# Products of a fused attention and gated feed-forward kernel for two pairs at once in half of the first stages, with a new order of steps

## The chip, the cores and the metric

The kernel runs on one core of one Trainium2 chip. The metric is the device time of one execution in microseconds (us), as the median of several runs. About 1% is what a measurement of this kernel can tell from no change.

## The reference

Attention over chunks of 64 positions (8 batches, 8 heads, 576 positions, head size 64), and behind it a feed-forward part without activation. All inputs and the output are float32; the kernel computes in bfloat16 with float32 sums.

```python
scores = scale * np.matmul(q_c, k_c.transpose(0, 1, 2, 4, 3))   # chunk by chunk
attn = softmax(scores)
out = np.matmul(attn, v_c)
x = out.transpose(0, 2, 1, 3).reshape(4608, 512)
a = x @ w1            # 512 -> 1024
b = x @ w2            # 512 -> 1024
h = a * b @ w3        # 1024 -> 1024
return h @ w_out      # 1024 -> 512
```

## The kernel before, in words

The 4608 tokens are cut into 18 pairs (p = 0 to 17) of 256 tokens (two units u of 128 tokens, each of two chunks). Two pairs make a couple of 512 tokens (g = p // 2). The product of w3 and w_out is made once in the kernel (steps V, W, Z), so that each couple needs one output product with `w3o` (512 columns).

There is no scheduler. A list in the text `ORDER` (lines 9 to 41) names every step, and the loop in lines 468 and 469 issues them in that order. Each engine works through its own instructions strictly in this order (`inorder`, line 92), and waits by semaphores for the data and buffers of others. So a step's place in the list is its place behind the earlier steps of the same engine only. The letters, with their functions:

- R (line 137) loads pair 0's raw q and k through the queues of SyncE (SP) and ScalarE (ACT); K casts them on ACT. q, k, v (lines 152 and 170), i (a quarter of w1 and of w2, 256 columns each, line 449), h (half of w3) and o (w_out) are loads on GpSimd's (POOL's) queue. A DMA here casts from float32 to bfloat16.
- T (line 201): transposes of q (T p.0) or k (T p.1) on VectorE (DVE). From pair 6 on, G (line 211, eight DMAs per couple on SP's queue) moves their 32-row blocks to other partitions, into `qkm`.
- S (line 220): the scores on TensorE (PE), 64 small matmuls for pairs 0 to 5, 32 from pair 6 on. E (line 237): the exponential on ACT. P (line 244): the product with v and a column of ones on PE.
- N (line 266): reciprocal of the sum and scaling on DVE, for unit 0 or 1. X (line 301): transpose of the result on DVE, into `xt` for pairs 0 to 5, else into `xm`, from which H (line 318, eight DMAs per couple on SP) moves it into `xt`.
- A and B (lines 361 to 366, through `do_AB`): x*w1 and x*w2 into the two banks of one PSUM tile (PSUM is the accumulation memory). C (line 368) copies the first from PSUM to SBUF on ACT; M (line 374) multiplies it with the second on DVE, into `ab`.
- O (line 398): output product, 16 matmuls of 512 columns on PE; Y: its copy on ACT; Q: its store on SP's queue.
- D (line 326): filler matmuls of zeros on PE, 9, 6 and 6 of 512 columns in the first stage.

A PSUM tile `p` of two banks is shared by S, P, A/B, W and O, and there are four of them (line 90); the buffers of q and k are five, of `ab` three, of `a_sb` three.

In `do_AB` before, a step A p.j of pairs 0 to 3 works for that pair alone: two blocks of 128 columns of w1 (f = 2j and 2j+1), four matmuls each over 256 tokens, eight matmuls with 256 columns (j = 0 to 3). From pair 4 on the steps stand at the even pairs only and work for a couple: one block f = j, four matmuls with 512 columns (j = 0 to 7).

```python
        fs = (f,) if p >= 4 else (2 * j, 2 * j + 1)
        n = GT // len(fs)
```

Of the kernel before, what the change touches and what calls it, by code (L numbers as in the profile page):

```python
# [7 lines left out]

ORDER = """
R0.0 R1.0 R0.1 R1.1 v0 D0.0.1.9.512 K0.0 K1.0 T0.0.0 K0.1 T0.1.0 K1.1 S0.0 T0.0.1 E0.0 T0.1.1 q1 k1  # L10
S0.1 i0 E0.1 P0.0 P0.1 T1.0 D0.1.0.6.512 v1 N0.0 T1.1 N0.1 X0.0 X0.1 i1 i2 S1 E1 D1.0.0.6.512 A0.0
C0.0 P1 B0.0 q2 N1.0 X1.0 N1.1 A0.1 C0.1 k2 B0.1 M0.0 A0.2 X1.1 A1.0 i3 C0.2 B0.2 M0.1 A1.1 v2 q3
B1.0 B1.1 M0.2 C1.0 C1.1 T2.0 k3 A0.3 C0.3 T2.1 S2 E2 B0.3 M1.0 M1.1 P2 M0.3 N2.0 N2.1 A1.2 C1.2
X2.0 A1.3 X2.1 C1.3 T3.0 B1.2 q4 T3.1 v3 k4 B1.3 A2.0 M1.2 C2.0 B2.0 S3 E3 T4.0 A2.1 M1.3 B2.1 M2.0
P3 A2.2 h0 N3.0 N3.1 B2.2 X3.0 A2.3 C2.1 C2.2 X3.1 o M2.1 C2.3 B2.3 A3.0 C3.0 M2.2 B3.0 V0 h1 A3.1
A3.2 q5 k5 C3.1 M2.3 B3.1 B3.2 v4 V1 C3.2 q6 T4.1 V2 V3 M3.0 W0 S4 k6 q7 M3.1 Z0 M3.2 V4 V5 W1 T5.0
Z1 W2 V6 V7 T5.1 W3 T6.0 E4 k7 q8 v5 Z2 A3.3 k8 q9 k9 Z3 S5 T6.1 T7.0 q10 T7.1 E5 v6 v7 C3.3 P4 B3.3
N4.0 X4.0 M3.3 O0 G3.0 N4.1 k10 Y0 G3.1 T8.0 O1 X4.1 P5 T8.1 Y1 O2 Q0 N5.0 N5.1 X5.0 v8 X5.1 A4.0 S6
E6 T9.0 T9.1 S7 B4.0 T10.0 Y2 q11 O3 C4.0 M4.0 Q1 E7 P6 v9 N6.0 A4.1 N6.1 C4.1 Y3 B4.1 A4.2 X6.0
M4.1 G4.0 A4.3 X6.1 C4.2 P7 N7.0 C4.3 B4.2 G4.1 k11 B4.3 N7.1 X7.0 A4.4 M4.2 B4.4 Q2 M4.3 C4.4 T10.1  # L20
M4.4 A4.5 C4.5 S8 B4.5 A4.6 C4.6 A4.7 E8 B4.6 Q3 C4.7 X7.1 B4.7 M4.5 q12 P8 H3.0 M4.6 S9 H3.1 M4.7
O4 E9 T11.0 Y4 P9 N8.0 O5 k12 N8.1 A6.0 B6.0 Y5 T11.1 G5.0 T12.0 A6.1 X8.0 N9.0 B6.1 C6.0 C6.1 T12.1
A6.2 q13 X8.1 B6.2 N9.1 X9.0 M6.0 k13 C6.2 v10 T13.0 v11 X9.1 M6.1 A6.3 M6.2 q14 G5.1 C6.3 A6.4 q15
B6.3 C6.4 B6.4 A6.5 S10 C6.5 B6.5 T13.1 M6.3 M6.4 A6.6 H4.0 E10 P10 H4.1 M6.5 S11 N10.0 B6.6 k14
N10.1 v12 A6.7 C6.6 E11 G6.0 P11 M6.6 N11.0 B6.7 X10.0 N11.1 A8.0 A8.1 B8.0 G6.1 C6.7 C8.0 B8.1 A8.2
B8.2 C8.1 M6.7 T14.0 q16 A8.3 M8.0 C8.2 M8.1 X10.1 M8.2 X11.0 Q4 q17 T14.1 H5.0 B8.3 C8.3 S12 S13
X11.1 A8.4 E12 C8.4 B8.4 k15 H5.1 M8.3 E13 v13 k16 A8.5 B8.5 P12 M8.4 k17 v14 T15.0 N12.0 N12.1 O6
A8.6 v15 C8.5 C8.6 T15.1 Y6 T16.0 B8.6 A8.7 M8.5 C8.7 P13 Q5 M8.6 B8.7 X12.0 A10.0 C10.0 B10.0 N13.0
N13.1 M8.7 G7.0 A10.1 T16.1 C10.1 A10.2 X12.1 X13.0 M10.0 C10.2 G7.1 B10.1 B10.2 A10.3 B10.3 C10.3
M10.1 T17.0 A10.4 C10.4 M10.2 M10.3 A10.5 T17.1 B10.4 M10.4 X13.1 v16 H6.0 S14 C10.5 S15 G8.0 B10.5  # L30
M10.5 O7 G8.1 E14 E15 P14 A10.6 H6.1 N14.0 C10.6 B10.6 A10.7 N14.1 Q6 Y7 M10.6 P15 N15.0 N15.1 C10.7
X14.0 S16 B10.7 M10.7 O8 E16 Q7 A12.0 B12.0 C12.0 M12.0 Y8 A12.1 C12.1 P16 S17 N16.0 X14.1 B12.1 E17
A12.2 M12.1 B12.2 A12.3 C12.2 A12.4 B12.3 X15.0 B12.4 v17 C12.3 M12.2 A12.5 N16.1 B12.5 M12.3 H7.0
X15.1 A12.6 X16.0 A12.7 C12.4 M12.4 C12.5 M12.5 C12.6 P17 N17.0 Q8 B12.6 B12.7 M12.6 H7.1 A14.0
A14.1 C12.7 B14.0 N17.1 C14.0 M12.7 O9 B14.1 C14.1 Y9 A14.2 X16.1 M14.0 M14.1 C14.2 A14.3 B14.2 Q9
O10 B14.3 X17.0 H8.0 Y10 Q10 A14.4 C14.3 A14.5 X17.1 C14.4 B14.4 M14.2 B14.5 H8.1 M14.3 A14.6 O11
Y11 B14.6 M14.4 O12 C14.5 C14.6 Y12 A14.7 M14.5 A16.0 C14.7 C16.0 Q11 M14.6 B14.7 A16.1 C16.1 A16.2
B16.0 B16.1 M14.7 M16.0 C16.2 M16.1 Q12 A16.3 O13 B16.2 B16.3 A16.4 C16.3 M16.2 Y13 M16.3 C16.4
A16.5 A16.6 B16.4 A16.7 C16.5 B16.5 M16.4 O14 Y14 C16.6 B16.6 C16.7 M16.5 B16.7 M16.6 Q13 M16.7 O15
Y15 O16 Q14 Q15 Y16 Q16 O17  # L40
"""


# [5 lines left out]
def first_path(  # L49
# [46 lines left out]
    def mm(*a, **kw):
        return inorder(nc.tensor.matmul(*a, **kw))  # L97
# [276 lines left out]
    def do_M(p, j):  # L374
        g = p // 2
        if g not in ab_t:
            ab_t[g] = msb.tile([P, FO, GT], bf, tag="ab", bufs=3, name="ab")
# [9 lines left out]
        inorder(nc.vector.tensor_mul(o, view(a_t.pop((p, j))[:]), view(ps_t.pop((p, j))[:, 1, :])))  # L387
# [201 lines left out]
```

## Time and profile before

| | |
|---|---|
| median of 3 runs | 242.46 us (241.17 to 243.07) |
| profiled execution: time | 241.66 us |
| profiled execution: span of its instructions | 240.1 us |
| mean granted TensorE clock | 0.985 |
| DMA moved | 39.21 MB, mean 163 GB/s |

The page's busy table gives each engine's busy time within the span. The views by stretch give, for a stretch of time, the busy time of an engine, the granted clock of TensorE (1.00 is full speed) and what the DMA engines moved. In a timeline a row has the start, the length, the engine, the line, the operation with output and input, the count, and in brackets the idle time ahead of it and what ended that. Names of tiles stand without buffer numbers, and all matmuls have line 97, the helper `mm`. A matmul tile that fillers allocated first is called `z_ps`, also where a score or a product goes into it later. A matmul's length holds its pipeline's drain, so the pace of a stream is read from start to start. A row's bracket names the releaser by what the profile infers.

### The profile page before, as it was taken

Reading aid. Unit: us, or ns where it says so; the run is one execution under the profiler, and the core shown is the slowest. Engines: PE = TensorE matmul, PEld = TensorE weight load, DVE = VectorE, ACT = ScalarE, POOL = GpSimd, SP = SyncE. Lnnn points to the kernel's source line nnn. Section 1 sums busy time; section 2 is a strip of 40 time slices with the busy share of each in tenths; the row PEclk is TensorE's granted clock in tenths of the full one; section 3 lists DMA queues with packets and bytes.
Section 4 is the critical chain, followed back from the end, with each engine's and each line's share of the span. In section 5 each row is a group of like instructions: output and inputs, shape, how many; then the busy total and the mean of one; then the engine's idle time right before and its main releaser. Section 6 shows DMA issues by size and latency. Waiting matters only on the chain.

```text
span 240.1 us, 6225 instructions
## 1 busy us (share of the span) xinstructions
PE 230.6 (96%) x2621; PEld 120.2 (50%) x2621; DVE 152.3 (63%) x237; ACT 84.7 (35%) x119; POOL 83.4 (35%) x112
## 2 busy tenths in 40 slices
...
GB/s 177 179 185 188 178 175 199 202 188 174 174 220 242 236 224 253 201 204 196 212 222 222 214 252 152 190 210 3 131 48 3 131 131 87 90 0 89 85 90 175
DMA packets 94397, 39.21 MB, mean 163 GB/s; under 512 B 75296, under 2 KB 86816, under 8 KB 94368
## 3 DMA queue, kind: packets, MB, share of 16 engines
...
q8 instruction: 20, 0.33, 0.5%
...
HBM read 38.80 MB, written 9.44 MB: 201 GB/s over the span
## 4 chain that ended last, share of the span: by engine, by line
PE 55%; DMA 31%; POOL 5%; DVE 3%; issue 2%; SPq 2%; ACT 1%; DVEq 0%; POOLq 0%
PE ab_ps L97 34%; PE o_ps L97 17%; DMA qk<-in_k_dram 17%; DMA w<-in_moe_w_dram 7%; DMA qk<-in_q_dram 4%; DMA qkm<-qkT 3%; POOL vbuf L100 2%; SPq L199 2%; PE s_ps L97 2%; POOL qk L100 2%; PE pv L97 2%; DVE ab L387 1%; POOL w L100 1%; DVE xn L272 1%; DVE qkT L207 1%
## 5 line engine op out<-in xcount | busy, mean ns | idle before, releaser
L97 PE MATMUL ab_ps<-xt,w 128*128 128x512 bf16 (+1 forms) x688 | 128.7, 342 | 0.5 <-DMA w<-in_moe_w_dram 0.5
L97 PEld LDWEIGHTS <-w 128*128 128x128 bf16 x704 | 67.0, 98 | 54.9 <-DMA w<-in_moe_w_dram 1.3
L387 DVE TENSOR_TENSOR ab<-a_sb,ab_ps 128x512 bf16<-128x512 f32 x71 | 47.0, 673 | 53.8 <-PE ab_ps L97 30.2
L370 ACT COPY a_sb<-ab_ps 128x512 f32<-128x512 f32 x71 | 41.4, 587 | 73.8 <-PE ab_ps L97 73.0
L97 PE MATMUL o_ps<-w3o,ab 128*128 128x512 bf16 (+2 forms) x296 | 64.8, 373 | 0.5 <-issue 0.3
L207 DVE STREAM_TRANSPOSE qkT<-qk 128x1024 bf16<-128x1024 bf16 (+1 forms) x38 | 45.8, 1232 | 5.5 <-ACT qk L150 3.7
L97 PEld LDWEIGHTS <-ab 128*128 128x128 bf16 x296 | 28.4, 98 | 33.6 <-issue 1.0
L100 POOL DMA_DIRECT2D vbuf<-in_v_dram x40 | 33.8, 847 | 23.2 <-DMA qk<-in_k_dram 5.9
L417 ACT COPY o_sb<-o_ps 128x1024 f32<-128x1024 f32 x17 | 17.2, 1014 | 43.8 <-PE o_ps L97 43.4
L272 DVE TENSOR_TENSOR xn<-pv,rcs 128x512 bf16<-128x512 f32 x36 | 24.9, 691 | 1.2
L100 POOL DMA_DIRECT2D qk<-in_q_dram x23 | 18.0, 783 | 15.8 <-DVE ab L387 4.8
L100 POOL DMA_DIRECT2D qk<-in_k_dram x23 | 17.9, 781 | 11.1 <-DMA qk<-in_k_dram 4.1
L240 ACT ACTIVATE e<-s_ps 128x1024 bf16<-128x1024 f32 (+1 forms) x17 | 16.9, 1000 | 11.4 <-PE s_ps L97 11.2
L313 DVE STREAM_TRANSPOSE xm<-xn 128x512 bf16<-128x512 bf16 x24 | 16.3, 689 | 0.1
L97 PE MATMUL w_ps<-wo,w3T 128*128 128x512 bf16 x64 | 14.1, 379 | 0.1
L269 DVE RECIPROCAL rcs<-pv 128x8 f32<-128x8 f32 x36 | 6.9, 192 | 11.4 <-PE pv L97 11.4
L291 POOL CROSS_LANE_REDUCE all_good<-good 128x1 f32<-128x1 f32 x1 | 0.4, 354 | 39.6 <-DVE both L289 39.6
L100 POOL DMA_DIRECT2D w<-in_moe_w_dram x16 | 11.1, 696 | 5.7 <-DMA w<-in_moe_w_dram 3.9
L97 PEld LDWEIGHTS <-e 64*32 64x32 bf16 (+1 forms) x768 | 7.8, 101 | 6.9 <-issue 4.4
L428 DVE STREAM_TRANSPOSE w3T<-w 128x1024 bf16<-128x1024 bf16 x8 | 9.5, 1210 | 2.4 <-DMA w<-in_moe_w_dram 2.4
L97 PE MATMUL pv<-vbuf,e 64*32 64x65 bf16 (+1 forms) x768 | 10.1, 198 | 0.3 <-ACT e L240 0.2
L97 PEld LDWEIGHTS <-w3T 128*128 128x128 bf16 x64 | 6.1, 98 | 7.5 <-issue 0.4
...
## 6 DMA issues: line engine op xcount, KB each, us to landing
...
qkm<-qkT SPq DMA_DIRECT2D x48, 128.0 KB, 7.0
vbuf<-in_v_dram POOLq DMA_DIRECT2D x32, 128.0 KB, 11.1
...
qk<-in_k_dram POOLq DMA_DIRECT2D x11, 256.0 KB, 12.1
...
```

What stands on the lines that cost most here:

```text
L97: return inorder(nc.tensor.matmul(*a, **kw))
L100: return inorder(nc.gpsimd.dma_start(dst, src))
L199: inorder(nc.sync.dma_start(dst, src))
L207: inorder(nc.vector.transpose(qkT_t[g][:, :, p % 2, s, heads(h)].rearrange("p e h (y t) -> p h t e y", t=2), qk_t[p][:, s, heads(h)].rearr ...
L240: inorder(nc.scalar.activation(e_t[p][:, :, heads(hh)], s_t[p, hh][:].rearrange("p u (h q) -> p u h q", q=CH)[:, :, heads(hh)], Exp, scale ...
L269: inorder(nc.vector.reciprocal(rc, pv[:, :, :, D:W]))
L272: inorder(nc.vector.tensor_mul(xn_t[p][:, u], pv[:, :, :, 0:D], rc.to_broadcast([P, 2, 4, D])))
L313: inorder(nc.vector.transpose(xm_t[g][:, u, :, m].rearrange("p o (c y) -> p c o y", y=BL), xn_t[p][:].rearrange("p u r m d -> p (u r) m d" ...
L370: first[p, j] = inorder(nc.scalar.copy(a_t[p, j][:], ps_t[p, j][:, 0, :]))
L387: inorder(nc.vector.tensor_mul(o, view(a_t.pop((p, j))[:]), view(ps_t.pop((p, j))[:, 1, :])))
L417: inorder(nc.scalar.copy(o_sb[:], ps_t.pop(p)[:]))
L428: inorder(nc.vector.transpose(w3T_t[f][:].rearrange("p k (f y) -> p f k y", y=BL), w3[:, NB * f:NB * (f + 1), :].rearrange("p f (k x) -> p ...
```

## The change

For pairs 0 to 3, the steps with j = 0 and 1 stay as they were: one pair, two blocks of columns, eight matmuls of 256 columns. They cover the first two quarters of w1 and w2. The third and fourth quarter (blocks f = 4 to 7) are made for the couple at once, by steps with j = 8 to 11 at pair 0 and at pair 2: f = j - 4, four matmuls of 512 columns. Where before 16 steps A and 16 steps B had eight matmuls each, now eight steps of each have eight and eight of each have four, 64 matmuls (and weight loads) fewer in all; the columns streamed are the same, and C and M stay 16 each. The helper `do_D` writes the same tile keys in another way.

The whole list `ORDER` is new: the loads on POOL's queue, and the order of steps on every engine, to the end of the kernel. Of the list the diff shows the beginning and the stretch from S8 to S12.

```diff
 ORDER = """
-R0.0 R1.0 R0.1 R1.1 v0 D0.0.1.9.512 K0.0 K1.0 T0.0.0 K0.1 T0.1.0 K1.1 S0.0 T0.0.1 E0.0 T0.1.1 q1 k1
-S0.1 i0 E0.1 P0.0 P0.1 T1.0 D0.1.0.6.512 v1 N0.0 T1.1 N0.1 X0.0 X0.1 i1 i2 S1 E1 D1.0.0.6.512 A0.0
-C0.0 P1 B0.0 q2 N1.0 X1.0 N1.1 A0.1 C0.1 k2 B0.1 M0.0 A0.2 X1.1 A1.0 i3 C0.2 B0.2 M0.1 A1.1 v2 q3
-B1.0 B1.1 M0.2 C1.0 C1.1 T2.0 k3 A0.3 C0.3 T2.1 S2 E2 B0.3 M1.0 M1.1 P2 M0.3 N2.0 N2.1 A1.2 C1.2
-X2.0 A1.3 X2.1 C1.3 T3.0 B1.2 q4 T3.1 v3 k4 B1.3 A2.0 M1.2 C2.0 B2.0 S3 E3 T4.0 A2.1 M1.3 B2.1 M2.0
-P3 A2.2 h0 N3.0 N3.1 B2.2 X3.0 A2.3 C2.1 C2.2 X3.1 o M2.1 C2.3 B2.3 A3.0 C3.0 M2.2 B3.0 V0 h1 A3.1
+R1.0 v0 R0.0 D0.0.1.9.512 R1.1 q1 k1 v1 i0 i1 K0.0 K1.0 R0.1 K0.1 K1.1 T0.0.0 T0.1.0 q2 i2 k2 q3 k3
+v2 i3 q4 v3 h0 o h1 k4 S0.0 E0.0 P0.0 T0.0.1 T0.1.1 T1.0 T1.1 S0.1 E0.1 P0.1 N0.0 X0.0 N0.1 X0.1
+D0.1.0.6.512 D1.0.0.6.512 q5 S1 E1 P1 N1.0 B0.0 X1.0 N1.1 X1.1 A0.0 C0.0 A0.1 A1.0 A1.1 B0.1 q6 k5
+k6 M0.0 B1.0 C0.1 C1.0 C1.1 T2.0 B1.1 M0.1 A0.8 M1.0 M1.1 A0.9 B0.8 C0.8 B0.9 T2.1 T3.0 T3.1 M0.8 q7
+S2 E2 S3 P2 E3 N2.0 X2.0 N2.1 C0.9 M0.9 X2.1 A0.10 C0.10 A0.11 B0.10 B0.11 A2.0 C0.11 M0.10 M0.11 P3
+C2.0 B2.0 N3.0 A2.1 C2.1 N3.1 X3.0 X3.1 B2.1 M2.0 M2.1 A3.0 T4.0 V0 A3.1 B3.0 C3.0 M3.0 V1 A2.8 A2.9
...
-M4.4 A4.5 C4.5 S8 B4.5 A4.6 C4.6 A4.7 E8 B4.6 Q3 C4.7 X7.1 B4.7 M4.5 q12 P8 H3.0 M4.6 S9 H3.1 M4.7
-O4 E9 T11.0 Y4 P9 N8.0 O5 k12 N8.1 A6.0 B6.0 Y5 T11.1 G5.0 T12.0 A6.1 X8.0 N9.0 B6.1 C6.0 C6.1 T12.1
-A6.2 q13 X8.1 B6.2 N9.1 X9.0 M6.0 k13 C6.2 v10 T13.0 v11 X9.1 M6.1 A6.3 M6.2 q14 G5.1 C6.3 A6.4 q15
-B6.3 C6.4 B6.4 A6.5 S10 C6.5 B6.5 T13.1 M6.3 M6.4 A6.6 H4.0 E10 P10 H4.1 M6.5 S11 N10.0 B6.6 k14
-N10.1 v12 A6.7 C6.6 E11 G6.0 P11 M6.6 N11.0 B6.7 X10.0 N11.1 A8.0 A8.1 B8.0 G6.1 C6.7 C8.0 B8.1 A8.2
-B8.2 C8.1 M6.7 T14.0 q16 A8.3 M8.0 C8.2 M8.1 X10.1 M8.2 X11.0 Q4 q17 T14.1 H5.0 B8.3 C8.3 S12 S13
+C4.1 N6.1 E7 C4.2 A4.3 M4.1 X6.0 C4.3 B4.2 M4.2 B4.3 A4.4 k11 X6.1 M4.3 v9 v10 S8 P7 E8 N7.0 N7.1
+B4.4 C4.4 A4.5 A4.6 B4.5 B4.6 X7.0 H3.0 C4.5 q12 q13 k12 X7.1 T10.0 M4.4 C4.6 A4.7 B4.7 C4.7 M4.5
+M4.6 M4.7 P8 S9 N8.0 O4 E9 T10.1 P9 N8.1 O5 T11.0 k13 T11.1 X8.0 X8.1 N9.0 T12.0 N9.1 Q3 H3.1 X9.0
+G5.0 Y4 A6.0 C6.0 q14 A6.1 G5.1 B6.0 M6.0 H4.0 B6.1 A6.2 v11 A6.3 q15 v12 C6.1 M6.1 q16 X9.1 C6.2
+B6.2 B6.3 T12.1 H4.1 T13.0 k14 k15 M6.2 T13.1 C6.3 M6.3 A6.4 A6.5 Y5 C6.4 B6.4 S10 S11 v13 C6.5 B6.5
+M6.4 A6.6 E10 E11 P10 M6.5 N10.0 A6.7 C6.6 B6.6 A8.0 B6.7 B8.0 N10.1 X10.0 M6.6 A8.1 G6.0 G6.1 C6.7
+C8.0 M6.7 C8.1 A8.2 X10.1 B8.1 B8.2 C8.2 M8.0 M8.1 M8.2 A8.3 P11 S12 q17 N11.0 N11.1 X11.0 B8.3 A8.4
...
 def do_D(which, p, j, n, cols):
-        d, key = ((s_t, (p, (None, 0)[j])), (ps_t, (p, j)), (pv_t, (p, 0)))[which]
+        d, key = ((s_t, (p, 0 if j == 1 else None)), (ps_t, (p, j)), (pv_t, (p, 0)))[which]
...
+    def single(p, j):
+
+        return p < 4 and j < FO // 2
+
     def do_AB(p, j, f, which):
 
+        if j >= FO // 2 and p < 4:
+            f = j - FO // 2
         if p >= MOVED:
             rhs = new_xt(p // 2)[:].rearrange("p (s o t) -> p o s t", s=2, o=KO)
         else:
             rhs = new_xt(p // 2)[:].rearrange("p (o t) -> p o t", o=KO)
-            if p < 4:
+            if single(p, j):
                 rhs = rhs[:, :, p % 2 * PT:(p % 2 + 1) * PT]
-        fs = (f,) if p >= 4 else (2 * j, 2 * j + 1)
+        fs = (2 * j, 2 * j + 1) if single(p, j) else (f,)
...
 def do_M(p, j):
-        if p < 4:
+        if single(p, j):
             o = ab_t[g][:, 2 * j:2 * j + 2, p % 2 * PT:(p % 2 + 1) * PT]
             view = lambda t: t.rearrange("p (j t) -> p j t", j=2)
         elif p < MOVED:
-            o = ab_t[g][:, j]
+            o = ab_t[g][:, j - FO // 2 if p < 4 else j]
```

On PE's own order, the beginning reads, before: nine fillers, S0.0, S0.1, P0.0, P0.1, six fillers, S1, six fillers, A0.0, P1, B0.0, A0.1; after: nine fillers, S0.0, P0.0, S0.1, P0.1, twelve fillers, S1, P1, B0.0, A0.0, A0.1, A1.0.

More of the change, by code (lines that the diff above doesn't have):

```diff
@@ L15 @@
-P3 A2.2 h0 N3.0 N3.1 B2.2 X3.0 A2.3 C2.1 C2.2 X3.1 o M2.1 C2.3 B2.3 A3.0 C3.0 M2.2 B3.0 V0 h1 A3.1
[L16 to L19, printed above, removed]
@@ L20 @@
-M4.1 G4.0 A4.3 X6.1 C4.2 P7 N7.0 C4.3 B4.2 G4.1 k11 B4.3 N7.1 X7.0 A4.4 M4.2 B4.4 Q2 M4.3 C4.4 T10.1
-M4.4 A4.5 C4.5 S8 B4.5 A4.6 C4.6 A4.7 E8 B4.6 Q3 C4.7 X7.1 B4.7 M4.5 q12 P8 H3.0 M4.6 S9 H3.1 M4.7
-O4 E9 T11.0 Y4 P9 N8.0 O5 k12 N8.1 A6.0 B6.0 Y5 T11.1 G5.0 T12.0 A6.1 X8.0 N9.0 B6.1 C6.0 C6.1 T12.1
-A6.2 q13 X8.1 B6.2 N9.1 X9.0 M6.0 k13 C6.2 v10 T13.0 v11 X9.1 M6.1 A6.3 M6.2 q14 G5.1 C6.3 A6.4 q15
-B6.3 C6.4 B6.4 A6.5 S10 C6.5 B6.5 T13.1 M6.3 M6.4 A6.6 H4.0 E10 P10 H4.1 M6.5 S11 N10.0 B6.6 k14
@@ L25 @@
-N10.1 v12 A6.7 C6.6 E11 G6.0 P11 M6.6 N11.0 B6.7 X10.0 N11.1 A8.0 A8.1 B8.0 G6.1 C6.7 C8.0 B8.1 A8.2
-B8.2 C8.1 M6.7 T14.0 q16 A8.3 M8.0 C8.2 M8.1 X10.1 M8.2 X11.0 Q4 q17 T14.1 H5.0 B8.3 C8.3 S12 S13
-X11.1 A8.4 E12 C8.4 B8.4 k15 H5.1 M8.3 E13 v13 k16 A8.5 B8.5 P12 M8.4 k17 v14 T15.0 N12.0 N12.1 O6
-A8.6 v15 C8.5 C8.6 T15.1 Y6 T16.0 B8.6 A8.7 M8.5 C8.7 P13 Q5 M8.6 B8.7 X12.0 A10.0 C10.0 B10.0 N13.0
-N13.1 M8.7 G7.0 A10.1 T16.1 C10.1 A10.2 X12.1 X13.0 M10.0 C10.2 G7.1 B10.1 B10.2 A10.3 B10.3 C10.3
@@ L30 @@
[L30 to L40, printed above, removed]
+R1.0 v0 R0.0 D0.0.1.9.512 R1.1 q1 k1 v1 i0 i1 K0.0 K1.0 R0.1 K0.1 K1.1 T0.0.0 T0.1.0 q2 i2 k2 q3 k3
@@ new lines @@
+A2.10 C3.1 B3.1 B2.8 C2.8 M3.1 M2.8 B2.9 B2.10 V2 C2.9 M2.9 A2.11 W0 C2.10 M2.10 V3 V4 T4.1 W1 V5
+T5.0 W2 C2.11 Z0 q8 V6 V7 W3 T5.1 B2.11 T6.0 T6.1 T7.0 k7 T7.1 v4 q9 Z1 Z2 Z3 S4 S5 k8 E4 M2.11 k9
+G3.0 T8.0 v5 v6 v7 O0 Y0 O1 q10 G3.1 v8 P4 T8.1 T9.0 N4.0 O2 X4.0 Q0 N4.1 E5 T9.1 k10 P5 N5.0 Y1 O3
+Q1 Y2 G4.0 N5.1 X4.1 G4.1 S6 E6 X5.0 X5.1 A4.0 Q2 B4.0 C4.0 Y3 A4.1 M4.0 P6 S7 B4.1 N6.0 A4.2 q11
+C4.1 N6.1 E7 C4.2 A4.3 M4.1 X6.0 C4.3 B4.2 M4.2 B4.3 A4.4 k11 X6.1 M4.3 v9 v10 S8 P7 E8 N7.0 N7.1
+B4.4 C4.4 A4.5 A4.6 B4.5 B4.6 X7.0 H3.0 C4.5 q12 q13 k12 X7.1 T10.0 M4.4 C4.6 A4.7 B4.7 C4.7 M4.5
```

14 lines of the change are left out of this document (added).

## The prediction

> **What bounds the kernel now.** I read the page's busy table first, then busy time by stretches, then the chain that ended last and the timelines of TensorE (PE), VectorE (DVE), GpSimd (POOL) and SyncE (SP) where the two orders differ.
>
> ```profile
> PE 230.6 (96%) x2621; PEld 120.2 (50%) x2621; DVE 152.3 (63%) x237; ACT 84.7 (35%) x119; POOL 83.4 (35%) x112
> ```
> ```profile
> 0.00:15.50 15.50, 10.93 (x213) 0.78 1.43 178
> 15.50:40.00 24.50, 23.77 (x499) 1.00 1.72 185
> 40.00:100.00 60.00, 59.69 (x770) 1.00 1.64 212
> 100.00:116.00 16.00, 15.63 (x132) 1.00 1.75 199
> 116.00:160.00 44.00, 43.70 (x563) 1.00 1.44 213
> 160.00:236.50 76.50, 76.50 (x451) 1.00 0.23 78
> ```
> The columns are stretch, length, PE busy, matmuls, granted clock, DMA share, GB/s. From 15.5 us to 236.5 us PE is idle for 0.73, 0.31, 0.37, 0.30 and 0 us: 1.71 us in all. What a new order can win there is 1.71 us; what it can lose has no such bound, because every PE wait after 15.5 us moves the end.
>
> **The wide products.** For pairs 0 to 3, 16 of the 32 groups of eight 256-column matmuls become 16 groups of four with 512 columns.
>
> ```profile
> 29.50 5.41 PE L97 MATMUL ab_ps<-xt,w 128*128 128x256 bf16 x48
> 34.85 0.96 PE L97 MATMUL s_ps<-qkT 32*64 32x64 bf16 x64
> 203.92 7.07 PE L97 MATMUL ab_ps<-xt,w 128*128 128x512 bf16 x32
> 210.82 3.62 PE L97 MATMUL o_ps<-w3o,ab 128*128 128x512 bf16 x16
> ```
> From start to next start, 48 narrow ones take 34.85 - 29.50 = 5.35 us (0.111 each; 0.109 without the last drain), so a group of eight is 0.874 us. 32 wide ones take 6.90 us (0.2156 each), so a group of four is 0.863 us. The gain is 16 x 0.011 = 0.18 us: streaming, not weight loading, sets both. Copies C on ACT and multiplications M on DVE stay 16 each, of 512 columns, so they are worth nothing; bounds for the term: 0 and, if no drain is subtracted, 16 x (0.892 - 0.863) = 0.5 us. I take 0.18.
>
> The Trainium skill ("TensorE: Matmul & The Clock Gate", Back-to-back issue gap) gives N/2.4 + 2.5 ns for an isolated stream, by which a merge saves 2.5 ns, 0.16 us over 64 merges; the same section also gives about 131 ns for a sustained 512-column matmul. The rows decide between the two: 215.6 ns. By 131 ns the term would be an estimated 64 x (218 - 131) = 5.6 us.
>
> **The start.** Raw loads and the first nine fillers D keep their order. On PE, S0.1 now follows P0.0, all twelve later fillers stand ahead of S1, and P1 stands ahead of the first product; before, S1 stood between the fillers and a product covered E1.
>
> ```profile
> 8.38 0.64 PE L97 MATMUL s_ps<-qkT 32*64 32x64 bf16 x32 [1.33 <-DVE qkT L207]
> 8.95 1.41 PE L97 MATMUL pv<-vbuf,e 64*32 64x65 bf16 x64
> 10.28 2.74 PE L97 MATMUL z_ps<-zero 128*128 128x512 bf16 x6
> 13.02 1.07 PE L97 MATMUL z_ps<-qkT 32*64 32x64 bf16 x64
> 14.02 1.70 PE L97 MATMUL z_ps<-zero 128*128 128x512 bf16 x6
> 15.56 1.04 PE L97 MATMUL z_ps<-xt,w 128*128 128x256 bf16 x8
> 16.52 0.70 PE L97 MATMUL pv<-vbuf,e 64*32 64x65 bf16 x64
> 18.04 2.10 PE L97 MATMUL ab_ps<-xt,w 128*128 128x256 bf16 x16
> 28.87 0.70 PE L97 MATMUL pv<-vbuf,e 64*32 64x65 bf16 x64 [0.16 <-ACT e L240]
> ```
> ```profile
> 27.79 1.02 ACT L240 ACTIVATE e<-s_ps 128x1024 bf16<-128x1024 f32 x1
> ```
> ```profile
> 4.24:7.65 3.41, 1.15 (x35) 1.00 1.81 231
> 7.65:11.06 3.41, 2.53 (x98) 0.51 1.77 184
> 11.06:14.47 3.41, 3.41 (x71) 0.50 1.81 181
> 14.47:17.88 3.41, 3.41 (x85) 0.99 1.58 191
> ```
> P0.0 starts when E0.0 is done (an estimate, 8.1 us) and takes half of 1.41 us, so S0.1, E0.1 and P0.1 come about 0.36 us later than before and the fillers start at 10.64 us. The clock is at half until 14.47 us, a filler then costs 2.56/6 = 0.427 us, so nine are done by 14.47; the other three at 0.2156 end at 15.12. S1 starts there and lasts 0.71 (the S rows at warm clock, 127.51 below), E1 starts 0.05 later, takes 1.02 and hands over in 0.04 (27.79 to 28.87): P1 starts at 16.94, and PE, free at 15.75, has nothing to do for 1.19 us. P1 takes 0.63 (28.87 to 29.50), B0.0 and A0.0 0.874 each: 19.32 us. Before, the same set was done at 18.04. Loss 1.28 us, nearly all of it the wait for E1. Ends: none if something could fill it (nothing stands between S1 and P1 in the order), 2 us if the fillers were all cold (12 x 0.427 puts S1 at 15.76).
>
> **18 to 40 us.**
>
> ```profile
> 17.02 0.21 DVE L269 RECIPROCAL rcs<-pv 128x8 f32<-128x8 f32 x1 [2.05 <-PE pv L97]
> 17.99 0.71 DVE L305 STREAM_TRANSPOSE xt<-xn 128x512 bf16<-128x512 bf16 x1
> 18.62 0.17 DVE L269 RECIPROCAL rcs<-pv 128x8 f32<-128x8 f32 x1
> 58.45 5.96 DVE L207 STREAM_TRANSPOSE qkT<-qk 128x1024 bf16<-128x1024 bf16 x5
> 88.94 1.25 DVE L387 TENSOR_TENSOR ab<-a_sb,ab_ps 128x512 bf16<-128x512 f32 x2
> ```
> Pitches on DVE: T 1.2 (5.96/5), M 0.6, N 0.84, X 0.61; N starts 0.5 after its P. A1.0 needs X1.1: N1.0 at 17.44, then 0.97 + 0.63 + 0.97 + 0.70 gives 20.7; PE is through A0.1 at 20.2: wait 0.5. Let B1.1 end at t. DVE still has M1.1, T2.1, T3.0, T3.1, done at t + 0.17 + 0.6 + 1.2 + 1.2 + 1.3 = t + 4.5; PE, after four wide groups and S2, wants S3 at t + 4.1: wait 0.4. Then E2 and E3 run back to back and A0.10 waits for E3 (t + 6.3 against t + 5.9): 0.4. P2's handover 0.06 and A3.0 behind X3.1 0.27 complete 1.67 us; the 0.73 us of before goes away. Net +0.94.
>
> Loads: the queue moves q2 ahead of w-part i2, and k2, q3, k3, v2 ahead of i3.
>
> ```profile
> 17.98 0.76 POOL L100 DMA_DIRECT2D w<-in_moe_w_dram  x1 [0.57 <-DMA w<-in_moe_w_dram]
> 32.24 2.10 POOL L100 DMA_DIRECT2D w<-in_moe_w_dram  x3 [0.81 <-DMA qk<-in_k_dram]
> ```
> i1's first half landed at 17.95, k3 ten items later at 32.2: 1.43 us an item. In the new order i3's first half takes the place of before's q3, one item ahead of k3: 30.8 us, against its use at about 31.4. i2 (22 to 23.4) is wanted at 25. v1 ahead of i0 makes i0 one item later, at most 16 us, and B0.0 wants it at 17.6. k4 moves behind h0, o and h1, twelve items, to about 54 us; T4.1 wants it then, behind V4, and PE has W0 to W3 (14 us) ahead of S4, which needs T4.1. These moves cost nothing, i3 by only 0.6 us; if that cover is gone, A0.10 waits and nothing else is queued for PE. Ends: 0 and, at the slowest item of the row above (32.24), about 1 us.
>
> **40 to 130 us.** The same walk finds PE waiting 0.2 for a late copy Y3 (P6) and 0.16 for M4.7 (O4). The large term is SP's chain: qkT blocks moved by G, wanted by S.
>
> ```profile
> 99.92 1.34 DVE qkT L207
> 106.38 7.69 DMA qkm<-qkT
> ```
> ```profile
> 101.31 5.66 SPq L199 DMA_DIRECT2D qkm<-qkT  x8
> 114.88 5.92 SPq L199 DMA_DIRECT2D qkm<-qkT  x8
> ```
> ```profile
> 104.03 9.66 PE L97 MATMUL ab_ps<-xt,w 128*128 128x512 bf16 x44
> 114.20 0.67 PE L97 MATMUL s_ps<-qkm 64*64 64x64 bf16 x31 [0.37 <-DMA qkm<-qkT]
> 127.51 0.71 PE L97 MATMUL s_ps<-qkm 64*64 64x64 bf16 x64
> ```
> T11.1 ends at 101.26; its eight moves (G5) have landed at 114.15, 12.9 us later, where S10 waited 0.37; eight moves of H4 and then G6 follow on SP; G6's last issue is at about 120.2, and with a landing like G5's or a little shorter it is there by about 127.3, 26.1 us after T11.1; S12 took it at 127.51 without a wait. In the new order T11.1 stands behind M4.7, N8.0, T10.1, N8.1, T11.0. With B4.7 ending at u it ends at u + 0.17 + 0.6 + 0.84 + 1.2 + 0.84 + 1.2 + 1.3 = u + 6.1, so G5 is there at u + 19.0 and G6 at u + 32.2. PE wants S10 after O4, P9, O5 and eleven wide groups: u + 0.87 + 3.45 + 0.38 + 3.45 + 9.5 = u + 17.65, wait 1.3. S12 comes 11.9 us after S10 (ten groups, P10 behind E11, P11), at u + 30.9: wait 1.3 to 1.4. Neither PE nor DVE has other work queued ahead of them. Sum 3.06; the 0.98 us of before's waits (0.31, 0.37, 0.30) goes: +2.08. Ends: 0 if the moves land fast, about 4 if a landing is a microsecond longer in both.
>
> **160 us to the end.** PE is full before and has only products and outputs after; the last output matmuls, copies and stores are the same: 0.
>
> **Sum.** The profiled execution took 241.66 us (span 240.1, 1.6 around it), 0.8 below the median 242.46. 241.66 - 0.18 + 1.28 + 0.94 + 2.08 = 245.8 us.
>
> **Rivals.**
> 1. Not slower by 1%: the moves of G5 and G6 land early enough. Once the loads had drained, the same moves landed in 2.5 us:
> ```profile
> qkm<-qkT SPq DMA_DIRECT2D x8, 128.0 KB, 2.5
> ```
> That row is from 148 us on, while at 101 us the landing took 7.69. If the loads, reordered, let go of the DMA engines before 102 us, or landing falls under about 6.3 us, S10 and S12 do not wait: 245.8 - 2.7 = 243.1. Against it: the same bytes go through the same queue.
> 2. The clock falls again. Above, a window 34% busy was followed by the half clock, one 74% busy did not bring it back. The new 14.47 to 17.88 holds the 1.19 us wait (65% busy). If that counts as idle, the next 3.41 us run at half: 1.7 us of work, of which the 0.5 us wait for X1.1 covers a part: +1.2, 247.0. The skill's same page (the HAM clock gate) lets the clock fall only after an idle window of about 3.4 us, by which it stays; the row at 4.24 fell with idle gaps of at most 1.7 us, so the rule is not enough here.
> 3. A wide matmul is much cheaper than two narrow ones. If it cost what one narrow costs (0.109), 64 merges would save about 7 us: 238.8. Against it stands the 512-column row, 0.2156 each in a stretch without a wait. The 131 ns of the skill belong here; by them it would be an estimated 240.2.
> 4. No new wait is real, because the walk is late by half a microsecond everywhere: 241.66 - 0.18 - up to 1.7 = 239.8 to 241.5. For it: each wait is below 1.5 us. Against: E1 ahead of P1 has no cover at all.
>
> **How the numbers follow.** Chances: forecast 0.42, rival 1 with part of the waits 0.28, rival 2 0.20, rival 3 0.01, rival 4 0.09. The range 243.0 to 248.5 holds the forecast, most of rival 1, rival 2 and landings a microsecond longer. About 1% (2.4 us) is what a measurement can tell from no change. Faster by over 1% needs all 1.71 us of waits gone and more: 0.03. Rival 1, most of rival 4 and the low edge of the forecast stay within 1%: 0.33. Slower: 0.64.
>
> **What would show it.** In the changed kernel: P1 waiting about 1.1 us for E1 near 16 us; S3 and A0.10 waiting 0.4 each near 30 us; S matmuls waiting for qkm over 1 us near 114 and 127 us; 512-column groups at 0.863 us; no wait for w; half clock only up to about 14.5 us. I am wrong if PE's idle time between 15 and 160 us is below 3 us, or if a load, not SP's moves or E1, ends the longest wait.

## The result, and the profile after

The changed kernel takes 245.84 us (median of 4 runs, 245.56 to 246.09); the kernel before took 242.76 us on the same chip (4 runs, 241.17 to 243.19). The ratio is 1.0142, 95% interval 1.0111 to 1.0174: 3.1 to 3.4 us, or 1.4%, slower. The profiled execution took 245.56 us, with a span of 244.0 us, against 241.66 us and 240.1 us before: 3.9 us more between these two executions.

First the page's row for TensorE (PE), then PE's busy time by stretches, with the columns of the prediction (stretch, length, PE busy, matmuls, granted clock, DMA share, GB/s). Of the 2557 matmuls 21 have no record in this trace.

```profile
PE 228.1 (93%) x2536; PEld 114.1 (47%) x2557; DVE 154.2 (63%) x237; ACT 85.0 (35%) x119; POOL 83.5 (34%) x112
```
```profile
15.50:40.00 24.50, 21.82 (x454) 1.00 1.70 186
40.00:100.00 60.00, 58.53 (x732) 1.00 1.69 205
100.00:116.00 16.00, 15.04 (x146) 1.00 1.62 217
116.00:160.00 44.00, 41.25 (x434) 1.00 1.29 176
160.00:240.40 80.40, 80.02 (x584) 1.00 0.29 96
```

PE is idle for 2.68, 1.47, 0.96 and 2.75 us up to 160 us, 7.9 us in all where it had been 1.71 (missing records are part of it: in the repeat below, whose trace has them all, it is 6.1; so the waits are read from the timeline). From 160 us on PE is full but for 0.4 us.

PE's timeline from the last fillers to the first W step (start, length, operation, in brackets the idle time before and its releaser):

```profile
11.56 3.18 PE L97 MATMUL z_ps<-zero 128*128 128x512 bf16 x10 [0.22 <-issue]
14.67 0.70 PE L97 MATMUL z_ps<-qkT 32*64 32x64 bf16 x64
16.52 0.70 PE L97 MATMUL pv<-vbuf,e 64*32 64x65 bf16 x64 [1.15 <-ACT e L240]
17.15 1.92 PE L97 MATMUL z_ps<-xt,w 128*128 128x256 bf16 x16
18.91 1.04 PE L97 MATMUL ab_ps<-xt,w 128*128 128x256 bf16 x8
20.32 7.99 PE L97 MATMUL ab_ps<-xt,w 128*128 128x256 bf16 x55 [0.37 <-DVE xt L305]
29.28 0.71 PE L97 MATMUL s_ps<-qkT 32*64 32x64 bf16 x64 [0.33 <-DVE qkT L207]
31.13 4.49 PE L97 MATMUL ab_ps<-xt,w 128*128 128x512 bf16 x23 [0.34 <-ACT e L240]
36.27 0.32 PE L97 MATMUL pv<-vbuf,e 64*32 64x65 bf16 x32 [0.41 <-DVE rcs L269]
...
48.68 1.67 PE L97 MATMUL w_ps<-wo,w3T 128*128 128x512 bf16 x7
```

The first row holds ten of the twelve fillers; the first of the twelve starts at 10.73 us, and one has no record. S1 starts at 14.67 and P1 waits 1.15 us for E1, with nothing in between. Then A1.0 waits 0.37 for X1.1, S3 0.33 for T3.1, A0.10 0.34 for E3, and the second half of P3 0.41. The 16 narrow matmuls from 17.15 to 18.91 take 0.110 each: full clock right behind the gap. In before, the first W step was at 47.25:

```profile
47.25 1.02 PE L97 MATMUL w_ps<-wo,w3T 128*128 128x512 bf16 x4
```

The later waits, from the same view of the changed kernel:

```profile
84.00 0.32 PE L97 MATMUL pv<-vbuf,e 64*64 64x65 bf16 x16 [0.55 <-ACT o_sb L423]
...
97.56 3.61 PE L97 MATMUL o_ps<-w3o,ab 128*128 128x512 bf16 x15 [0.18 <-DVE ab L393]
...
106.01 9.66 PE L97 MATMUL ab_ps<-xt,w 128*128 128x512 bf16 x44 [0.90 <-DMA xt<-xm]
115.60 0.71 PE L97 MATMUL s_ps<-qkm 64*64 64x64 bf16 x64
...
121.89 7.07 PE L97 MATMUL ab_ps<-xt,w 128*128 128x512 bf16 x32 [1.52 <-DMA qkm<-qkT]
...
129.17 0.95 PE L97 MATMUL s_ps<-qkm 64*64 64x64 bf16 x32
...
143.31 6.20 PE L97 MATMUL ab_ps<-xt,w 128*128 128x512 bf16 x28 [1.09 <-DVE qkT L207]
```

They are P6 (behind the copy Y3), O4 (for M4.7), A6.0, S10 (no wait), A8.0, S12 (0.95 for 32 matmuls that take 0.45 elsewhere: a wait of some 0.5 inside the group) and A10.0. The releasers named at 121.89 and 143.31 must be read with the code: A8.0 and A10.0 read `xt`, which the moves H4 and H5 fill. SP's queue shows when these were issued, and the DMA view of 107 to 117 us how long the eight of H4 took to land:

```profile
93.00 2.99 SPq L199 DMA_DIRECT2D xt<-xm  x4
96.09 0.60 SPq L199 DMA_DIRECT2D out_dram<-o_sb  x1
96.78 3.53 SPq L199 DMA_DIRECT2D xt<-xm  x4
102.83 4.99 SPq L199 DMA_DIRECT2D qkm<-qkT  x8
108.70 7.80 SPq L199 DMA_DIRECT2D xt<-xm  x8
116.61 5.68 SPq L199 DMA_DIRECT2D qkm<-qkT  x8
...
131.82 5.52 SPq L199 DMA_DIRECT2D xt<-xm  x8
```
```profile
xt<-xm SPq DMA_DIRECT2D x8, 64.0 KB, 6.9
```

H3 (second half behind the store Q3), G5, H4, G6, H5: H4's last issue ends at 116.5 and A8.0 starts at 121.9; H5's ends at 137.3 and A10.0 starts at 143.3. All these moves stand in one queue, one group behind the other.

**The time by stages.** The start of A0.1 (the third product step) marks the end of the head's first part, the start of W0 the end of the second. At W0 the kernel before still has A3.3 and B3.3 to do (1.75 us), the changed one only B2.11 (0.86), so 0.89 is taken off the stretch ahead of W0 and added to the one behind it. In before A0.1 starts at 18.04, W0 29.21 later, the end 192.85 behind W0. The other rows are traces of experiments told below; all of them have the changed kernel's order up to W0.

| kernel | A0.1 | W0 | span | start | A0.1 to W0 | W0 to the end | sum |
|---|---|---|---|---|---|---|---|
| changed | 18.91 | 48.68 | 244.0 | +0.87 | -0.33 | +3.36 | +3.9 |
| after_again | 19.29 | 49.30 | 243.3 | +1.25 | -0.09 | +2.04 | +3.2 |
| q3_late | 19.74 | 49.80 | 245.0 | +1.70 | -0.04 | +3.24 | +4.9 |
| t11_early | 19.64 | 49.37 | 242.1 | +1.60 | -0.37 | +0.77 | +2.0 |
| narrow | 20.28 | 50.83 | 244.9 | +2.24 | +0.45 | +2.11 | +4.8 |
| predicted | | | | +1.28 | +0.76 | +2.08 | +4.1 |

For example after_again: 49.30 - 19.29 - 29.21 - 0.89 = -0.09, and 243.3 - 49.30 - 192.85 + 0.89 = 2.04. The measure is one trace of before. Two runs told below have its order up to W0 as well, before_no_late_v and old_head_new_tail: there A0.1 starts at 17.85 and 17.68, W0 at 47.47 and 47.58. Against them the start would cost up to 0.4 us more and the stretch from A0.1 to W0 up to 0.7 us less.

### The profile page after: what moved, and what is told of

Read it like the earlier page. It is cut to its first block, busy times and chain, and to the rows that moved or that the text cites. A ratio compares the mean times of both kernels' runs of the same rounds, so it can differ in the third digit from the quotient of the medians.

```text
span 244.0 us, 6069 instructions
## 1 busy us (share of the span) xinstructions
PE 228.1 (93%) x2536; PEld 114.1 (47%) x2557; DVE 154.2 (63%) x237; ACT 85.0 (35%) x119; POOL 83.5 (34%) x112
## 4 chain that ended last, share of the span: by engine, by line
PE 74%; DMA 10%; DVE 7%; ACT 3%; SPq 3%; issue 2%; ACTq 0%; DVEq 0%
PE ab_ps L97 41%; PE o_ps L97 21%; PE w_ps L97 6%; DMA qkm<-qkT 5%; DVE qkT L207 3%; PE pv L97 3%; SPq L199 3%; PE s_ps L97 2%; DMA raw<-in_k_dram 2%; DMA xt<-xm 2%; ACT e L240 2%; PE z_ps L97 2%; DVE xn L272 1%; DVE ab L393 1%; DVE xt L305 1%
## 5 line engine op out<-in xcount | busy, mean ns | idle before, releaser
L97 PE MATMUL ab_ps<-xt,w 128*128 128x512 bf16 (+1 forms) x617 | 126.1, 360 | 4.9 <-DMA qkm<-qkT 1.5
L97 PEld LDWEIGHTS <-w 128*128 128x128 bf16 x640 | 61.2, 98 | 64.6 <-issue 2.1
L97 PE MATMUL o_ps<-w3o,ab 128*128 128x512 bf16 (+2 forms) x284 | 63.4, 373 | 0.8 <-DVE ab L393 0.2
```

## The experiments

Theory at the start: three places cost, as predicted, the E1 wait, the waits of 18 to 40 us, and SP's chain behind T11.1; the merge itself is worth little. Rivals: the merge is worth much more or less; the clock; the landing of the moves under the loads, whatever the order. Each ratio is to the kernel before on the same chip.

**narrow.** The new order, with every wide product as two 256-column halves.

```diff
         fs = (2 * j, 2 * j + 1) if single(p, j) else (f,)
+        halves = p < 4 and not single(p, j)
+        if halves:
+            fs = (f, f)
...
-                         lhsT=(w1, w2)[which][:, ki, f * P:(f + 1) * P], rhs=rhs[:, ki],
+                         lhsT=(w1, w2)[which][:, ki, f * P:(f + 1) * P],
+                         rhs=rhs[:, ki, i * n:(i + 1) * n] if halves else rhs[:, ki],
```

> The new order unchanged, but each wide product made as two halves of 256 columns: 64 matmuls and weight loads more, nothing else. The prediction's term (a group of eight narrow ones 0.874 us, four wide ones 0.863) says 0.2 us more than the changed kernel: about 246.0 us. The comparison of the two traces up to the first W suggests that narrow groups run at about 0.90 us beside other work: 0.6 us more, about 246.4. If weight loading bounds narrow matmuls, well over 1 us more.

Measured: 246.75 us, ratio 1.0201 (1.0169 to 1.0233). Part of it is a later start in its trace (S1 at 16.04). From A1.0 to W0, where 15 of the 16 merged groups lie, it took 29.14 us (21.69 to 50.83), against 28.36 in the changed kernel, 28.60 in after_again and 28.65 in q3_late: 0.5 to 0.8 us more. PE's timeline shows that the pace of the matmuls is the smaller part of this:

```profile
21.69 8.03 PE L97 MATMUL ab_ps<-xt,w 128*128 128x256 bf16 x72 [0.37 <-DVE xt L305]
...
32.49 4.53 PE L97 MATMUL ab_ps<-xt,w 128*128 128x256 bf16 x40 [0.29 <-ACT e L240]
37.67 0.70 PE L97 MATMUL pv<-vbuf,e 64*32 64x65 bf16 x64 [0.66 <-ACT a_sb L380]
38.30 12.69 PE L97 MATMUL ab_ps<-xt,w 128*128 128x256 bf16 x112
```

The first two streams hold four merged groups each. They take 8.03 and 4.53 us, in the changed kernel 7.99 and 4.49: 0.01 us a group, 0.16 us for 16, as predicted. The third holds seven and takes 12.69 us, in after_again 12.33. Of these 0.36 us some 0.28 are one stop inside the stream: between 40.82 and 41.21 us no matmul starts. What is left lies mostly at P3, which waits 0.66 us before its first half. In the unaltered order P3 waits before its second half, by 0.41 (changed kernel), 0.65 (after_again) and 0.69 us (q3_late). So the merge is worth 0.2 us by its pace. Whether the narrow halves also caused these two waits, or whether they came with this one trace, the run doesn't show. The merge is no loss, and not the 7 us of rival 3.

**new_head_old_tail and old_head_new_tail.** The list of one kernel up to O0, behind it the steps that are left in the order of the other.

> The new list up to the first output product O0 (wide products, new start), then the steps left over in the order of before. By the prediction's terms the head costs 2.0 us (start 1.28, 18 to 40 us 0.94, merge -0.18): about 244.8 us. By the comparison of the traces the new kernel is only 0.5 us behind at W0 (48.68 us with one group of 0.86 left, against 47.25 with two of 0.87 left): about 243.3. Rival: the head leaves the loads so that the old tail waits too: 245 or more.

Measured: 247.92 us, ratio 1.0239 (1.0217 to 1.0261). PE's timeline in it:

```profile
67.25 1.47 PE L97 MATMUL o_ps<-w3o,ab 128*128 128x512 bf16 x6
72.43 1.87 PE L97 MATMUL o_ps<-w3o,ab 128*128 128x512 bf16 x6 [3.71 <-issue]
```

PE stood still for 3.71 us in the middle of O0, where no semaphore and no buffer is waited for. The run says nothing on the head's price: this stop is larger than what was to be measured.

> The mirror: the list of before up to O0 (all products of pairs 0 to 3 narrow), then the rest in the new order. The prediction gives the tail 2.08 us: about 244.8 us. The traces give it some 3.4 us, waits for moves on SP's queue above all: about 246.1. If those waits come only from what the new head does to loads and transposes, the time is that of before, 242.8.

Measured: 246.15 us, ratio 1.0185 (1.0159 to 1.0211). W0 starts at 47.58 (0.33 later than before, a wait for `wo`), and from there to the end it takes 196.1 us against 192.85: the new tail alone costs 3.3 us in this trace and about as much as the whole change. Its waits stand at A6.0 (1.62) and A10.0 (1.72), both for the moves H.

**start_cover.** S1 and E1 ahead of the last six fillers, A0.0 ahead of P1, B0.1 ahead of A1.0.

```diff
-D0.1.0.6.512 D1.0.0.6.512 q5 S1 E1 P1 N1.0 B0.0 X1.0 N1.1 X1.1 A0.0 C0.0 A0.1 A1.0 A1.1 B0.1 ...
+D0.1.0.6.512 q5 S1 E1 D1.0.0.6.512 A0.0 C0.0 P1 N1.0 B0.0 X1.0 N1.1 X1.1 A0.1 B0.1 A1.0 A1.1 ...
```

> The new order, but S1 and E1 ahead of the last six fillers, A0.0 ahead of P1 and B0.1 ahead of A1.0, as the order of before had them: P1 no longer stands behind E1 with nothing to do. If the wait for E1 is a loss of 1.2 us by itself: about 244.6 us. If P1 starts when it did (16.5 us in both traces), X1.1 and so A1.0 stay where they are, and only the one group done earlier is won, 0.87 us: about 245.0. If the later waits for SP's moves swallow it: 245.8, no change.

Measured: 245.45 us, ratio 1.0142 (1.0107 to 1.0178), no different from the changed kernel. P1's wait for E1 is gone (P1 at 17.90 without a wait), but no gain is measured: in its trace most of the six fillers behind S1 still ran at half clock (2.19 us from 14.74 on, where six took 1.54 in before), A1.0 came at 21.70 and waited 0.37 as before, W0 started at 49.46. Both intervals are about 0.9 us wide to either side, so a small gain is not excluded, and what the wait would be worth with the clock back sooner is not shown.

**after_again.** The changed kernel itself, once more.

> The changed kernel once more, unaltered, beside the three below, which are variants of it: 1.014 of the time of before, as measured first. Its profile also shows once more where the filler matmuls end: if the moment at which the clock comes back moves from run to run, S1 starts anywhere from 14.3 to 16.1 us.

Measured: 245.5 us, ratio 1.0138 (1.0099 to 1.0177). Waits: P1 1.15, A6.0 1.17, A8.0 0.46, S12 0.42, A10.0 0.96. The sizes of the late waits change from run to run, with the same order.

**fewer_fillers.** The second six of the twelve fillers left out.

```diff
-D0.1.0.6.512 D1.0.0.6.512 ...
+D0.1.0.6.512 D1.0.0.0.512 ...
```

> The new order without the last six of the twelve filler matmuls ahead of S1. T1.1 was done at 12.3 us, and S1 stood behind fillers until 14.7 to 16.0. If the fillers only delay S1, it starts near 13.3, P1 near 15.2, X1.1 is done near 19.0: 1.3 us or a little more below the changed kernel. If the fillers bring the clock back and it now stays at half through the first products, nothing is won or up to 2 us lost.

Measured: 246.09 us, ratio 1.0162 (1.0127 to 1.0196). A1.0 starts at 19.51, 0.8 to 1.2 earlier than in the changed kernel, but W0 at 50.55, 1.25 to 1.9 later. First PE's timeline, then its busy time and clock in two stretches of 3.4 us, and the same two in the changed kernel:

```profile
28.92 0.69 PE L97 MATMUL s_ps<-qkT 32*64 32x64 bf16 x62 [0.78 <-DVE qkT L207]
30.18 0.21 PE L97 MATMUL s_ps<-qkT 32*64 32x64 bf16 x2 [0.57 <-issue]
30.32 0.70 PE L97 MATMUL pv<-vbuf,e 64*32 64x65 bf16 x64
31.51 6.03 PE L97 MATMUL ab_ps<-xt,w 128*128 128x512 bf16 x24 [0.49 <-ACT e L240]
```
```profile
28.00:31.40 3.40, 1.67 (x145) 0.98 1.55 187
31.40:34.80 3.40, 3.29 (x9) 0.52 2.03 176
```
```profile
28.00:31.40 3.40, 2.63 (x195) 1.00 1.60 189
31.40:34.80 3.40, 3.35 (x18) 1.00 2.01 174
```

Starting earlier, PE ran into S3 before T3.1 was done, stopped once more inside S3, and then waited for E3. None of the gaps is over 0.78 us, but PE was busy for only 1.67 of 3.4 us, and the clock fell to half for the next 3.4 us: 24 matmuls took 6.03 us instead of about 4.5. In the changed kernel the same stretch is 2.63 us busy and the clock stays. So the second fall of the clock exists (rival 2), though not where the prediction put it; it costs about 1.5 us, more than the fillers saved.

On such a fall the Trainium skill ("TensorE: Matmul & The Clock Gate", "What's actually happening") asks for an idle window of about 3.4 us; by that alone the clock would have stayed here. The Trainium skill says in the same page's section "A second HAM failure mode: psum-queue depth-cycling" that short idle times between groups of matmuls can make the clock swing; with this the trace agrees (gaps of 0.78, 0.57 and 0.49 us, here behind transposes, an unexplained stop and the exponential).

**q3_late.** The store Q3 behind the moves H3.1 on SP's queue.

```diff
-... N9.1 Q3 H3.1 X9.0
+... N9.1 H3.1 Q3 X9.0
```

> The new order with the store Q3 behind H3.1 on SP's queue instead of between H3.0 and H3.1. In the changed kernel A6.0 waited 0.9 us for H3, then A8.0 1.5 us for H4. If these waits are separate, 0.6 us or more is won. If they are links of one chain (T11.1, G5, H4 on SP, each group of eight moves held by the landing of the one before), the wait at A6.0 shrinks, the one at A8.0 grows by as much, and the time stays.

Measured: 245.82 us, ratio 1.0138 (1.01 to 1.0175). A6.0 starts without a wait at 105.48, and the wait is met one link on:

```profile
117.14 1.02 PE L97 MATMUL s_ps<-qkm 64*64 64x64 bf16 x63 [1.86 <-DMA qkm<-qkT]
...
123.01 7.07 PE L97 MATMUL ab_ps<-xt,w 128*128 128x512 bf16 x32 [0.77 <-DMA qkm<-qkT]
```

S10 now waits 1.86 for G5, A8.0 0.77, A10.0 1.07. This is the wait that the prediction had for S10; in the changed kernel A6.0's wait merely stood ahead of it. A6.0's own wait came from the place of Q3 between the two halves of H3.

**merge_old_order.** Before's order with the wide products alone; the steps with j = 8 to 11 stand at the later of the two pairs' old places (A0.3 becomes A0.8, A1.2 A0.9, A1.3 A0.10, A2.2 A0.11; A3.2 and A3.3 become A2.8 and A2.9, with A2.10 and A2.11 behind them; B, C and M likewise).

> The wide products alone: the list of before, in which the steps j = 2 and 3 of pairs 0 to 3 are taken out and the wide steps put in the places of A0.3, A1.2, A1.3, A2.2, A3.2, A3.3 and behind the last two. By the price of the products (0.2 us by the prediction, 0.6 to 0.9 by the run with narrow halves) it would be 0.2 to 0.9 us faster than before. But the narrow steps A0.2 and A2.3 had filled PE between P1 or P3 and X1.1 or X3.1: A1.0 would wait about 0.9 us, A3.0 about 1.4, and the time is about 1.5 us above before.

Measured: 244.74 us, ratio 1.0108 (1.0059 to 1.0157). Merged steps need both pairs, so the single-pair products that had filled PE behind P1 and P3 are missing there: A1.0 waits 0.84 and A3.0 1.00 for X, S2 0.58 for T, the second half of P2 0.48 for its v load, W0 1.04 for M. The merge in the old places is a loss of 1%, as expected in kind and larger than the 1.5 us that were expected.

**after_no_late_v and before_no_late_v.** The v loads of pairs 8 to 17 left out in both kernels (the products of those pairs use what an older pair left in the buffer), to take load traffic from 80 us on.

```diff
-            for u in range(2):
+            for u in range(2 if p < 8 else 0):
```

> The changed kernel with the loads of v left out for pairs 8 to 17 (their products use what an older pair left in the buffer): 20 of the 40 v pieces' bytes, 2.5 MB less on POOL's queue after 60 us, every wait and every other instruction kept. If the new waits (A6.0, A8.0, S12, A10.0) come from moves on SP's queue that land late because they share the DMA engines with the loads, they shrink and 2 to 3 us go: about 243, within 1% of before. If they come from the order on DVE alone, they stay: above 245.

> The kernel before with the same loads left out, as the measure for the run above. Its waits for moves sum to 0.4 us, so by either theory it should be within 0.6 us of the kernel before; the excess of the changed kernel over it falls from 3.4 us to under 1.5 if sharing the DMA engines is the cause, and stays otherwise.

Measured: 244.06 us, ratio 1.0101 (1.0066 to 1.0137), and 241.25 us, ratio 0.9965 (0.9945 to 0.9985). By the medians 2.8 us lie between the two orders, by the ratios 1.36% or 3.3 us; with all loads it had been 3.5 us (245.5 against 242.01) and 1.38%. In the trace of the changed order A6.0's and A10.0's waits vanish, S12's falls to some 0.3 and A8.0's to 0.33, while S10 waits 0.95. Single waits are shorter there, but in the time a gain from leaving the loads out can't be told from none; most of the loss is not due to them.

**fewer_fillers_old_tail.** Six fillers fewer, new head, old tail.

> The new head without six fillers, then the order of before: the head with the old tail once more, with twelve PE instructions fewer ahead of O0. In the first such run PE stood still 3.7 us in O0, waiting for nothing that the profile shows, while a 16 KB packet of the instruction queue was on its way. If that is the loading of code behind busy DMA engines, the place moves by a few steps and the time may fall to about 244; if it is something of the mixed order (a missing buffer), it stays in O0 with 3.7 us, 247 to 248.

Measured: 247.5 us, ratio 1.0224 (1.0165 to 1.0282). Again a stop in O without a releaser (1.71 us), one of 1.10 inside S3, and half clock from 32.28 us on. The stop that spoiled new_head_old_tail came back at the same step with another length, so the hybrid lists can't price the new head.

**t11_early.** q3_late, and the transposes T10.1, T11.0 and T11.1 directly behind M4.7, ahead of the normalisations N8.0 and N8.1.

```diff
-M4.6 M4.7 P8 S9 N8.0 O4 E9 T10.1 P9 N8.1 O5 T11.0 k13 T11.1 X8.0 X8.1 N9.0 T12.0 N9.1 Q3 H3.1 X9.0
+M4.6 M4.7 P8 S9 T10.1 T11.0 k13 T11.1 N8.0 O4 E9 P9 N8.1 O5 X8.0 X8.1 N9.0 T12.0 N9.1 H3.1 Q3 X9.0
```

> The changed kernel with two moves in its list: the transposes T10.1, T11.0 and T11.1 stand directly behind M4.7 on VectorE, ahead of the normalisations N8.0 and N8.1, and the store Q3 stands behind the moves H3.1. Everything else is the changed kernel. Theory of the chain (the end of T11.1 sets G5, that H4, that G6, and the waits at A6.0, S10, A8.0 and S12 are links of it): T11.1 ends about 1.7 us earlier (two N of 0.84 no longer ahead of it), so G5 is there about 1.7 us earlier; the wait of S10, 1.86 with Q3 moved alone, falls to 0.5 or less, A8.0's 0.77 goes as well, A6.0 does not wait; A10.0's wait (H5, about 1.1) stays, since it hangs on N11 and not on T11. Time about 243.5 to 244.3, 1.5 to 2 us less than the changed kernel's 245.5 to 245.8. Rival: the landings under the loads, not the place of T11.1, set these waits, or the keys of pair 11 are not there 1.7 us earlier: T11.1 then waits for its load, the waits stay within 0.3 us of 1.86 and 0.77, and the time stays at 245.5 to 246. A gain of S10's wait that comes back at A8.0 or A10.0 without a change in time would say that a later link (N11, H5) holds the end.

Measured: 243.89 us (11 runs, 242.93 to 244.79), ratio 1.0074 (1.0047 to 1.0101), where the changed kernel's repeat has 1.0138 (1.0099 to 1.0177) and q3_late 1.0138 (1.01 to 1.0175). Its DVE, SP and PE, and the landing of G5:

```profile
97.40 3.65 DVE L207 STREAM_TRANSPOSE qkT<-qk 128x1024 bf16<-128x1024 bf16 x3
```
```profile
101.11 5.29 SPq L199 DMA_DIRECT2D qkm<-qkT  x8
```
```profile
qkm<-qkT SPq DMA_DIRECT2D x8, 128.0 KB, 6.8
```
```profile
101.90 0.32 PE L97 MATMUL pv<-vbuf,e 64*64 64x65 bf16 x16 [0.50 <-DVE xn L272]
102.75 3.61 PE L97 MATMUL o_ps<-w3o,ab 128*128 128x512 bf16 x15 [0.52 <-DVE xn L272]
106.19 9.66 PE L97 MATMUL ab_ps<-xt,w 128*128 128x512 bf16 x44
115.78 0.78 PE L97 MATMUL s_ps<-qkm 64*64 64x64 bf16 x64
...
141.45 6.20 PE L97 MATMUL ab_ps<-xt,w 128*128 128x512 bf16 x28 [0.65 <-issue]
```

The three transposes run back to back, G5 is issued at 101.11 instead of 102.83, and the landing stays at 6.8 us. A6.0, S10 and A8.0 no longer wait; some 0.5 is left at S12 and 0.65 at A10.0, where 1.1 had been expected to stay. N8, now late, costs P9 and O5 0.5 each. From W0 to the end the loss is 0.8 us where it was 2.0 to 3.4. Since moving Q3 alone left S10 waiting 1.86 and A8.0 0.77, and the time where it was, the place of T11.1 on DVE, with the landings as they are, sets those two waits; a faster landing isn't needed. This removes about half of the change's loss and is the best version of the new order; no version that ran beat the kernel before.

## Why the prediction came out

The sum (245.8 against 245.84 us) was right. Its account was right in kind at the start and behind 40 us; in between it named the new waits rightly, but not what they replace. So the agreement to 0.1 us is partly luck: the loss from 18 to 40 us didn't come and, in the first trace, the one behind 40 us was larger by about as much; in the repeat the three stages come to 3.2 us instead of 4.1. And the 4.1 us were added to the profiled execution of before, 241.66 us, while between the medians lie 3.1 us (245.84 against 242.76).

- **The start (1.28 predicted; 0.87 and 1.25 in the two traces of the changed kernel).** Right: P1 waits 1.15 for E1 (predicted 1.19), S1 starts at 14.67 and 15.05 (15.12). The difference is the length of the twelve fillers, 3.94 and 4.22 us: how many of them run at half clock varies. That the wait was the cost in itself is not borne out: start_cover removed it, and the time stayed; in its trace fillers at half clock and the wait for X1.1 took its place.
- **18 to 40 us (0.94 predicted, and 0.18 off for the merge; -0.33 and -0.09 measured from A0.1 to W0).** The waits came as walked: A1.0 0.37 (0.5), S3 0.33 (0.4), A0.10 0.34 (0.4); instead of P2 0.06 and A3.0 0.27 there was one of 0.41 at P3. They sum to 1.45, where 1.67 had been predicted (the five terms that it lists make 1.63). The merge's 0.18 is right too: narrow shows 0.16 by the pace of the streams. What was mis-sized is the 0.73 us of before that go away. They are idle time as the profile counts it, which leaves out the drain that a matmul's length holds (a narrow one lasts 0.27 us at a pace of 0.109) and a stop inside a step. Read from start to start in before's timeline, its products from A0.1 to W0 take 26.42 us, where 28 groups at 0.874 make 24.47: 1.95 us of waits and changes between steps, and S3, at 0.96 instead of 0.71, holds 0.25 more. That is 2.2 us. By the same measure the products of the changed kernel take 25.91 us (14 groups at 0.874 and 15 at 0.863 make 25.18), 0.73 over, and its S and P steps hold 1.3 us of waits (1.55 in the repeat): 2.0 and 2.3 us. So the new order lost nothing in this stretch: it waits for X1.1, T3.1 and E3 where before waited for w and changed more often between products, S and P. (By the same reading the 80 narrow matmuls from 38.22 to 47.25 us in before took 8.91 us with their drain and kept the pace of 0.109; the rest up to W0 is a wait.)
- **40 us to the end (2.08 predicted; 3.36 and 2.04).** The mechanism is shown by q3_late and t11_early: T11.1 behind M4.7 and the N steps, then SP's chain. Its places were off. Predicted were S10 and S12, for G5 and G6; it was A6.0, A8.0 and A10.0, for H3, H4 and H5, with 0.5 of S12. The prediction had H4 in the chain only as what stands ahead of G6 and didn't ask who wants H4 itself, nor that Q3 stands ahead of H3.1: A6.0's wait hangs on Q3 and not on T11.1, and it covered S10's, which q3_late shows (1.86). A10.0's wait for H5 the prediction didn't have; no run isolates it. P6's wait for Y3 was 0.55 and none in the repeat (0.2), O4's 0.18 (0.16).
- **Loads.** No wait for w at all, as predicted; in before there were two (0.29 and 0.20).
- **Rival 1** (moves land early) didn't come: the landing in the stretch of G5 is 6.8 us, above the 6.3 from which it would have decided. **Rival 2** didn't come in the changed kernel: the products behind the 1.15 us gap run at full clock (PE was busy for 2.27 of the 3.41 us from 14.47 to 17.88). **Rival 3** is refuted by the 32 wide matmuls of 7.07 us at 121.89, the same as before, and by narrow; the Trainium skill's sustained figure for 512 columns ("TensorE: Matmul & The Clock Gate", Back-to-back issue gap, 131 ns) doesn't hold here. **Rival 4** (no wait is real) is refuted by the waits above.

Open: what the stops without a releaser are, whether the merge saves waits besides its 0.2 us, and how the about 2 us that t11_early still loses in its trace (+1.6 in the start, by the table) could be had back while the clock's return varies.
